# A new order table and new choices among equal engines in an attention and feed-forward kernel on one core

## The chip, the core and the metric

The kernel runs on one core of a Trainium2 chip. A core has five engines that work side by side, each through its own queue of instructions: TensorE (PE in the profile) multiplies matrices, VectorE (DVE), ScalarE (ACT) and GpSimd (POOL) work on elements, and SyncE (SP) here issues the transfers (DMA). Instructions of different engines wait for one another on semaphores. The metric is the device time of one execution in microseconds. The kernel before takes 1097.91 us (median of three runs, 1097.19 to 1097.92).

## The reference

Two parts follow one another. The first is attention with a threshold, over 8 batches, 8 heads, 576 positions and 64 channels a head; q, k and v are float32:

```python
scores = scale * np.matmul(q, k.transpose(0, 1, 3, 2))
thresh = np.max(scores, axis=-1, keepdims=True) - tau
scores = np.where(scores >= thresh, scores, -1000000000.0)
scores = scores - np.max(scores, axis=-1, keepdims=True)
attn = np.exp(scores)
attn = attn / (np.sum(attn, axis=-1, keepdims=True) + 1e-09)
return np.matmul(attn, v).astype(np.float32)
```

Its output, with the heads side by side, is x of 4608 tokens by 512. The second part is a feed-forward layer whose weights come as float64 (w_in 512 x 2048, w_out 2048 x 512): h = x @ w_in; g = h where h >= 1, 0 where h <= -1, (h + 1)^2 / 4 between; the output is g @ w_out.

## The kernel before, in words

**Numbers.** Products are made in float16 with a high and a low part of each factor (three products, high by high, high by low and low by high). A helper on line 466 issues most matmuls, so the feed-forward products of both kinds stand under that line: with `ph` as output the product x @ w_in, 144 steps of 48 matmuls (or parts of it), with `acc` as output the product g @ w_out, 264 steps. The q and k of the first four head pairs, all of batch 0, are used in float32 as they come ("exact", `f32` in a row), so that no split stands ahead of the first scores.

**Weights.** They arrive in 16 blocks for w_in and 16 for w_out, 128 x 512 float64 or 0.524 MB each (line 839). The float64 words are turned into float32 on lines 845 to 874: a letter for each block in `SIGN` (A, D or N) says which engines do it (A: ScalarE twice and VectorE once; D: GpSimd, ScalarE, VectorE twice; N: ScalarE, GpSimd, VectorE). After scales that come from all blocks (sums on line 881), a letter in `CONV` says how a block is scaled and split into high and low parts (lines 920 to 958):

- A: ScalarE scales and rounds (lines 922 and 928), GpSimd subtracts. G: all three on GpSimd.
- D: GpSimd scales and rounds in one (line 936), VectorE makes the residual from the block in SBUF (line 939).
- P and Q: GpSimd as in D, TensorE makes the residual (line 942), and ScalarE (P, line 949) or VectorE (Q, line 947) reads it from PSUM. M: TensorE scales, ScalarE rounds, VectorE subtracts.

**q and k after batch 0.** They are loaded in head pairs into `raw` and scaled and split by `add_qk`. A letter of `QHOW` says how: P (GpSimd line 645, ScalarE line 651, GpSimd line 658) or D (ScalarE line 649, VectorE line 656). v is scaled on line 728 (GpSimd) with its residual on line 733 (VectorE) for 28 head pairs; the first come as float32.

**Attention.** The scores are made in 288 tiles of 128 rows by 576 columns, two tiles to a visit (144 visits). `PAIR` says whether TensorE makes both tiles interleaved (J, one step) or one after the other (S, two steps) on line 1073. Each tile then goes: row maximum (VectorE line 1127), threshold (one column; VectorE line 1134, or ScalarE line 1132 where `THR` says A), exponential (ScalarE line 1137), mask and sum (VectorE line 1151), and then by its letter in `TILE`:

- P, where no letter stands: 1/sum (VectorE line 1161), norm (GpSimd line 1169), high part (ScalarE line 1177), low part (GpSimd line 1180).
- N: the same but the norm on ScalarE (line 1172), and VectorE's 1/sum has two short instructions (lines 1203 and 1204).
- V: high part with its norm on ScalarE (line 1207), low part on VectorE (line 1210). S is a form of V that works on the scores' own buffer (lines 1188 to 1199).

SyncE transposes the result (line 1213, tile `eT`), and TensorE multiplies it by v (line 1299). The sum goes to x on lines 1307 and 1311; x @ w_in goes through the gate on ScalarE and VectorE (lines 1376 to 1393), is multiplied by w_out and stored.

**Order.** All work is written down as 5016 operations on five engines, each with the operations that it follows and the buffers that it takes. The table `ORDER` lists them; `Plan.order` goes through the table, gives each operation its buffer slots and a planned time, and sorts by that. Each engine executes its operations in this sequence, so a step that waits holds all behind it on its engine. A last helper, `keep_warm` (line 1454), fills TensorE's planned gaps in the first 120 us with matmuls on a constant, 314 instructions before. The x @ w_in steps run through groups of 256 tokens: the first step of the second group is an event to which the prediction comes back, at 161.56 us.

Of the kernel before, what the change touches and what calls it, by code (L numbers as in the profile page):

```python
# [26 lines left out]
CONV = {"i": "AGAGGAGGPAGAADDP", "o": "PDDAADMGAAQGAGAD"}  # L27

SIGN = {"i": "NNNAADANAAANANAA", "o": "AAAANANAAANANNNN"}
THR = "VVAVVVVVVVAAVVAAAAAAAAAAVAVVVVAVVVAAVVAAVVAAVVVVAAAAVVAVVVVVVVVVVVVVVVVVVVVVVVVVVVVVVVVVVVVVVVVVVVVVVVVVVVVVVVVVVVVVVVVVVVVVVVVVVVVVVVVVVVVVVVVVVVVVVVVVVVVVVVVVVVVVVVVVVVVVVVVVVVVVVVVVVVVVVVVVVVVVVVVVVVVVVVVVVVVVVVVVVVVVVVVVVVVVVVVVVVVVVVVVVVVVVVVVVVVVVVVVVVVVVVVVVVVVVVVVVVVVVVVVVVVVVVVV"  # L30
PAIR = "SJSJSJSSJSSSSJJJJJSJJJJJJJJJJJJSJJJJJJJJJJJJJJJJJJJJJJJJJJJJJJJJJJJJJJJJJJJJJJJJJJJJJJJJJJJJJJJJJJJJJJJJJJJJJJJJJJJJJJJJJJJJJJJJJJJJJJJJJJJJJJJJ"
QHOW = "DDPDPPDPPPDDPPPPPPPPPPPPPDDPPPPP"
# [216 lines left out]
TILE = {3: "S", 5: "N", 8: "N", 18: "V", 20: "N", 22: "N", 25: "V", 26: "N", 27: "N", 29: "V", 30: "N", 32: "N", 55: "V", 69: "V", 71: "V", 94: "V", 114: "V", 117: "V", 150: "V", 152: "V", 173: "V", 181: "V", 186: "V", 200: "V", 214: "S", 222: "V", 257: "V", 262: "V", 287: "V"}  # L249
# [1261 lines left out]
```

## Time and profile before

| | |
|---|---|
| time, median of three runs | 1097.91 us |
| span of the profiled execution | 1097.3 us |
| TensorE busy | 1073.0 us (98%) |
| TensorE weight loads | 790.6 us (72%) |
| VectorE busy | 906.1 us (83%) |
| ScalarE busy | 871.2 us (79%) |
| GpSimd busy | 759.4 us (69%) |

The profiled execution has no other time than its span, which lies 0.6 us under the median. A busy share over the whole span mixes stages: the weights are converted only at its start, the attention ends well before its end, and TensorE's busy time contains the filler matmuls. It must be read by stretches of time, and the waits too.

### The profile page before, as it was taken

What the parts mean: (1) busy time and instruction counts of PE and PEld (TensorE: products, weight loads), DVE (VectorE), ACT (ScalarE), POOL (GpSimd) and SP (SyncE); (2) the same over time, 40 slices, a digit from 0 to 9 for tenths busy, and PEclk for the clock granted to TensorE, in tenths of its full rate; (3) what the DMA queues carried; (4) which work ended last, traced back from release to release, by engine and by line L of the source; (5) the groups of instructions that cost most, each with busy time, mean ns of one, the idle gap of its engine ahead of it and who ended that gap; (6) DMA issues with size and microseconds to landing.
All of it is one profiled execution on the core that took longest, in us unless ns stands there. A gap on an engine that the chain in (4) does not pass through costs nothing.

```text
span 1097.3 us, 36713 instructions
## 1 busy us (share of the span) xinstructions
PE 1073.0 (98%) x14591; PEld 790.6 (72%) x14591; DVE 906.1 (83%) x2651; ACT 871.2 (79%) x1682; POOL 759.4 (69%) x880
## 2 busy tenths in 40 slices
PE   8799999999999999999999999999999999999998
PEld 7477668777777777776777677777786677767774
DVE  5899999999888888988898998888887899877223
ACT  5999989897888897887798888778788986776333
POOL 5999998786678785897668776576567885565000
PEclk9799999999999999999999999999999999999999
DMA  9997899775977887787778788569856676557000
GB/s 352 332 256 143 139 188 141 152 140 115 191 140 141 152 152 127 135 150 137 139 142 146 150 128 147 113 127 164 151 102 120 131 128 127 105 95 132 18 15 20
DMA packets 420668, 155.88 MB, mean 142 GB/s; under 512 B 399504, under 2 KB 399504, under 8 KB 420496
## 3 DMA queue, kind: packets, MB, share of 16 engines
q1 hardware_dynamic: 420416, 153.41, 71.7%
q8 instruction: 114, 1.87, 0.7%
q14 instruction: 58, 0.48, 0.2%
q10 hardware_dynamic: 80, 0.13, 0.0%
HBM read 45.09 MB, written 9.44 MB: 50 GB/s over the span
## 4 chain that ended last, share of the span: by engine, by line
PE 80%; DVE 10%; DMA 5%; POOL 2%; issue 2%; ACT 1%; SPq 0%; DVEq 0%; POOLq 0%; ACTq 0%
PE acc L466 30%; PE ph L466 30%; PE s L1073 9%; PE ph L1299 9%; DMA eT<-hl 2%; DVE s L1127 2%; DVE e L1151 2%; POOL hl L1180 1%; PE ph L1454 1%; DMA qq<-in_q_dram 1%; DMA kk<-in_k_dram 1%; DMA raw<-in_v_dram 1%; DVE ph L1383 1%; POOL e L1169 0%; DVE WO L939 0%
## 5 line engine op out<-in xcount | busy, mean ns | idle before, releaser
L466 PEld LDWEIGHTS <-WI 128*64 128x64 f16 (+1 forms) x7446 | 407.3, 108 | 55.1 <-issue 18.3
L1180 POOL TENSOR_TENSOR hl<-e,hl 128x576 f16<-128x576 f32 x267 | 347.3, 1309 | 107.7 <-ACT hl L1177 101.8
L466 PE MATMUL ph<-x,WI 128*64 128x256 f16 (+1 forms) x6912 | 400.6, 264 | 2.3 <-DVE x L1311 0.9
L1169 POOL TENSOR_SCALAR e<-e,sm 128x576 f32<-128x576 f32 x259 | 203.5, 790 | 106.6 <-DVE sm L1161 75.3
L1151 DVE SCALAR_TENSOR_TENSOR e<-s,sm,e 128x578 f32<-128x578 f32 x286 | 229.9, 812 | 21.6 <-ACT e L1137 17.0
L1137 ACT ACTIVATE e<-s,sm 128x576 f32<-128x576 f32 x288 | 208.5, 739 | 40.4 <-DVE s L1127 36.4
L1127 DVE TENSOR_SCALAR_CACHE_REDUCE s<-s,pc 128x576 f32<-128x576 f32 x252 | 203.5, 820 | 36.6 <-PE s L1073 35.3
L1177 ACT ACTIVATE hl<-e 128x576 f16<-128x576 f32 x267 | 178.2, 680 | 44.1 <-POOL e L1169 41.1
L466 PE MATMUL acc<-WO,ga 128*64 128x512 f16 (+1 forms) x1590 | 203.4, 380 | 0.0
L1073 PE MATMUL s<-kk,qq 64*128 64x288 f16 (+3 forms) x1840 | 152.1, 300 | 9.9 <-DMA qq<-in_q_dram 5.2
L466 PEld LDWEIGHTS <-ga 128*64 128x64 f16 (+1 forms) x1590 | 91.2, 109 | 82.3 <-issue 9.9
L1383 DVE SCALAR_TENSOR_TENSOR ph<-ph,fcs,asq 128x512 f32<-128x512 f32 (+1 forms) x160 | 111.7, 700 | 46.1 <-ACT asq L1379 44.9
L1376 ACT ACTIVATE asq<-ph,fcs 128x512 f32<-128x512 f32 (+1 forms) x160 | 116.1, 736 | 37.7 <-PE ph L466 36.9
L1299 PE MATMUL ph<-eT,vst 128*64 128x320 f16 (+2 forms) x1928 | 122.7, 279 | 2.9 <-DMA eT<-hl 2.0
L1299 PEld LDWEIGHTS <-vst 128*64 128x64 f16 x1928 | 100.2, 110 | 22.9 <-issue 7.9
L1073 PEld LDWEIGHTS <-qq 64*128 64x128 f16 (+1 forms) x1680 | 66.2, 96 | 48.3 <-issue 35.6
L1388 ACT ACTIVATE ga<-ph,fcs 128x256 f16<-128x256 f32 (+1 forms) x160 | 70.2, 450 | 29.2 <-DVE ph L1383 22.4
L1379 ACT ACTIVATE asq<-asq 128x512 f32<-128x512 f32 x144 | 90.3, 629 | 3.2
L1393 DVE SCALAR_TENSOR_TENSOR ga<-ph,fcs,ga 128x256 f16<-128x256 f32 (+1 forms) x160 | 70.5, 449 | 23.7 <-ACT WI L1388 8.3
L466 PE MATMUL acc<-WO,gb 128*64 128x512 f16 (+1 forms) x546 | 71.0, 379 | 0.0
L466 PE MATMUL acc<-WO 128*64 128x512 f16 (+1 forms) x546 | 69.4, 380 | 0.0
L466 PE MATMUL acc<-WO,WI 128*64 128x512 f16 (+1 forms) x534 | 68.2, 380 | 0.0
(189 smaller groups left out, 1162.5 us busy)
## 6 DMA issues: line engine op xcount, KB each, us to landing
raw<-in_v_dram SPq DMA_DIRECT2D x32, 288.0 KB, 3.5
WO<-in_moe_w_in_dram SPq DMA_DIRECT2D x16, 512.0 KB, 8.6
out_dram<-ob SPq DMA_DIRECT2D x32, 256.0 KB, 2.8
raw<-in_q_dram SPq DMA_DIRECT2D x28, 288.0 KB, 3.4
raw<-in_k_dram SPq DMA_DIRECT2D x28, 288.0 KB, 3.5
x<-in_moe_w_out_dram SPq DMA_DIRECT2D x10, 512.0 KB, 7.0
eT<-hl SPq DMA_TRANSPOSE x288, 3.5
WO<-in_moe_w_out_dram SPq DMA_DIRECT2D x4, 512.0 KB, 4.3
```

The source lines that it names most:

```text
L466: T.matmul(out[x], lhsT[:, x], rhs, **flags)
L1073: T.matmul(ap(sb, s_ps)[r, f, :SH], q, k, start=ql == kl == 0, stop=exact or ql == 1)
L1127: V.tensor_scalar(sv(), sv(), c, None, ALU.mult, ALU.min, accum_out=t[:, 0:1])
L1137: A.activation(ev(), sv(), AF.Exp, bias=ap(m, sm)[:, 0:1], scale=-1.0)
L1151: V.scalar_tensor_tensor(ev(SH + 1), sv(SH + 1), t[:, 2:3], ev(SH + 1), ALU.is_le, ALU.mult, accum_out=t[:, 3:4])
L1169: G.tensor_scalar(ev(), ev(), ap(m, sm)[:, 5:6], ESC, ALU.mult, ALU.mult)
L1177: A.activation(part2(0), ev(), AF.Copy)
L1180: G.tensor_tensor(part2(w), ev(), part2(0), ALU.subtract)
L1299: T.matmul(o[hd * D : (hd + 1) * D, :n], vt[:, k, hd * D : (hd + 1) * D], t[:, kb, (hd ^ p % 2) * n : ((hd ^ p % 2) + 1) * n], start=m == ...
L1376: A.activation(tv()[:, :, c], hv()[:, :, c], AF.Relu, bias=fcs[:, b, 2, q : q + 1], scale=fcs[:, b, 3, q : q + 1])
L1379: A.activation(ap(tb, asq), ap(tb, asq), AF.Square)
L1383: V.scalar_tensor_tensor(hv()[:, :, c], hv()[:, :, c], fcs[:, b, 0, q : q + 1], tv()[:, :, c], ALU.max, ALU.min)
```

## The change

The table of all 5016 operations is another one, the letters of which engine does an operation are others, and `QHOW` now has one letter for q and one for k of each head pair where it had one for both. No operation and no buffer is new in kind. Of `ORDER`, which is 198 lines of numbers, the first line stands here; of `THR` 23 of its letters change (26 letters A before, 27 after), and it is left out.

```diff
-CONV = {"i": "AGAGGAGGPAGAADDP", "o": "PDDAADMGAAQGAGAD"}
-SIGN = {"i": "NNNAADANAAANANAA", "o": "AAAANANAAANANNNN"}
+CONV = {"i": "AGAGGAGGPAGAADDP", "o": "QDAAADMGGAQGAGAD"}
+SIGN = {"i": "NNAAADNNAAAAANAA", "o": "AADANANAAANANNNN"}
...
-PAIR = "SJSJSJSSJSSSSJJJJJSJJJJJJJJJJJJSJJJJJJJJJJJJJJJJJJJJJJJJJJJJJJJJJJJJJJJJJJJJJJJJJJJJJJJJJJJJJJJJJJJJJJJJJJJJJJJJJJJJJJJJJJJJJJJJJJJJJJJJJJJJJJJJ"
-QHOW = "DDPDPPDPPPDDPPPPPPPPPPPPPDDPPPPP"
+PAIR = "SSSSSJSSJSSSJSJJJJJJJJJJJJJJJJJJJJJJJJJJJJJJJJJJJJJJJJJJJJJJJJJJJJJJJJJJJJJJJJJJJJJJJJJJJJJJJJJJJJJJJJJJJJJJJJJJJJJJJJJJJJJJJJJJJJJJJJJJJJJJJJJJ"
+QHOW = "DDDDPPDDPPPPDPPPPPPPDPPPPPDPPPPDPPPPPPPPDDPPPPPPPPDDDDPPPPPPPPPP"
...
-    0, 605, 606, 607, 608, 609, 12, 16, 13, 17, 1, 14, 18, 15, 19, 20, 21, 590, 592, 22, 23, 595, 580, 582, 591, 585, 587, 2, 593, 600, 611, 616, 596,
+    585, 12, 16, 14, 0, 1, 13, 15, 17, 586, 587, 588, 18, 19, 20, 590, 21, 591, 22, 23, 39, 605, 592, 593, 606, 607, 608, 40, 24, 41, 42, 43, 580,
...
-TILE = {3: "S", 5: "N", 8: "N", 18: "V", 20: "N", 22: "N", 25: "V", 26: "N", 27: "N", 29: "V", 30: "N", 32: "N", 55: "V", 69: "V", 71: "V", 94: "V", 114: "V", 117: "V", 150: "V", 152: "V", 173: "V", 181: "V", 186: "V", 200: "V", 214: "S", 222: "V", 257: "V", 262: "V", 287: "V"}
+TILE = {3: "S", 5: "N", 8: "N", 18: "V", 20: "N", 22: "N", 25: "V", 26: "N", 27: "N", 29: "V", 30: "N", 32: "N", 37: "N", 55: "N", 62: "N", 65: "N", 69: "V", 71: "V", 72: "N", 73: "V", 85: "N", 90: "N", 94: "V", 96: "N", 99: "N", 101: "V", 107: "N", 109: "N", 110: "V", 111: "N", 114: "V", 117: "V", 119: "N", 146: "V", 147: "N", 151: "N", 153: "N", 154: "V", 157: "N", 164: "N", 173: "V", 174: "N", 181: "V", 186: "V", 200: "V", 214: "S", 222: "V", 257: "V", 262: "V", 287: "V"}
...
-            for how in plan.ways(("qk", at), QHOW[at], "PD"):
+            for how in plan.ways(("qk", 2 * at + n), QHOW[2 * at + n], "PD"):
```

Counted by instructions: line 1169 goes from 259 to 238, line 1172 from 8 to 27, lines 1203 and 1204 from 27 to 48, lines 1207 and 1210 from 19 to 21, line 1177 from 267 to 265, the fillers of line 1454 from 314 to 310; line 939 from 6 to 5 (on w_out from 4 to 3), line 947 from 1 to 2, line 949 from 3 to 2, line 874 from 1 to 2. `QHOW` has 46 letters P and 10 letters D on q and k after batch 0, in both kernels. TensorE's useful matmuls are the same. Of the 717 steps on TensorE about 217 stand elsewhere, none by more than 16 places.

Three places in the new order follow, each before and after. The first is SyncE's queue at its start. `WO` in a load is the buffer of a weight block, `x` also holds weight blocks at first, `kk` and `qq` are k and q of a head pair, `tcs` is the constant tau. Before:

```order
L571 DMA kk_76<-in_k_dram 128x576
L571 DMA qq_80<-in_q_dram 128x576
L839 DMA WO<-in_moe_w_in_dram 128x1024 x3
L571 DMA qq_81<-in_q_dram 128x576
L571 DMA kk_77<-in_k_dram 128x576
L839 DMA WO<-in_moe_w_in_dram 128x1024
L839 DMA x_107<-in_moe_w_out_dram 128x1024
L839 DMA x_105<-in_moe_w_out_dram 128x1024
L839 DMA WO<-in_moe_w_in_dram 128x1024 x3
L571 DMA kk_78<-in_k_dram 128x576
L571 DMA qq_82<-in_q_dram 128x576
```

After:

```order
L839 DMA WO<-in_moe_w_in_dram 128x1024 x7
L571 DMA kk_76<-in_k_dram 128x576
L571 DMA qq_80<-in_q_dram 128x576
L513 DMA tcs<-in_tau_dram 128x1
L839 DMA WO<-in_moe_w_in_dram 128x1024
L571 DMA qq_81<-in_q_dram 128x576
L571 DMA kk_77<-in_k_dram 128x576
L839 DMA WO<-in_moe_w_in_dram 128x1024 x3
L839 DMA x_107<-in_moe_w_out_dram 128x1024
L571 DMA qq_82<-in_q_dram 128x576
L571 DMA kk_78<-in_k_dram 128x576
```

The third pair's q (`qq_82`) stood behind 17 weight loads (8 of them stand ahead of the first row shown) and now stands behind 13 (one ahead of the first row); the four that were ahead now come later.

The second place is VectorE's queue at about 100 to 110 us of the trace of before, where w_out is split: line 939 makes a residual of a block, line 947 reads one from PSUM, line 1127 and 1151 are the maxima and masks of tiles, 1383 is a gate step, 1311 the low part of x. Before:

```order
L1151 SCALAR_TENSOR_TENSOR e_90,sm_126<-s_62,sm_126,e_90 128x578
L1311 SCALAR_TENSOR_TENSOR x_103<-ph_63,x_103 128x128
L939 SCALAR_TENSOR_TENSOR WO<-WO,wsc_o 128x512
L1161 RECIPROCAL sm_126<-sm_126 128x1
L1127 TENSOR_SCALAR s_61,sm_125<-s_61,tcs 128x2x288
L1127 TENSOR_SCALAR s_62,sm_127<-s_62,tcs 128x2x288
L939 SCALAR_TENSOR_TENSOR WO<-WO,wsc_o 128x512
L1210 SCALAR_TENSOR_TENSOR hl_96<-e_91,sm_123,hl_96 128x576
L1151 SCALAR_TENSOR_TENSOR e_89,sm_125<-s_61,sm_125,e_89 128x578
```

After:

```order
L947 TENSOR_SCALAR WO<-ph_64 128x512
L1151 SCALAR_TENSOR_TENSOR e_89,sm_125<-s_61,sm_125,e_89 128x578
...
L1311 SCALAR_TENSOR_TENSOR x_103<-ph_65,x_103 128x128
L1210 SCALAR_TENSOR_TENSOR hl_94<-e_92,sm_123,hl_94 128x576
L1127 TENSOR_SCALAR s_61,sm_127<-s_61,tcs 128x2x288
L1383 SCALAR_TENSOR_TENSOR ph_63<-ph_63,fcs,asq_101 128x512
L1127 TENSOR_SCALAR s_62,sm_126<-s_62,tcs 128x2x288
L1151 SCALAR_TENSOR_TENSOR e_92,sm_127<-s_61,sm_127,e_92 128x578
L1161 RECIPROCAL sm_127<-sm_127 128x1
L939 SCALAR_TENSOR_TENSOR WO<-WO,wsc_o 128x512
L1151 SCALAR_TENSOR_TENSOR e_90,sm_126<-s_62,sm_126,e_90 128x578
```

One of the two residuals of line 939 is gone from this stretch, and one more of line 947 stands some rows ahead.

The third place is TensorE's queue around the attention product that begins at 414.10 us of the trace of before. `s` is a score tile's PSUM buffer, `eT_98` the transposed tile, `vst_86` v, `WI` and `WO` hold weights in a feed-forward product and `gb_114` a gated result. Before:

```order
L466 LDWEIGHTS WI
L466 MATMUL ph_65<-x_104,WI 64x2x128
L1073 LDWEIGHTS qq_81
L1073 MATMUL s_61<-kk_77,qq_81 128x288
...
L1299 LDWEIGHTS vst_86
L1299 MATMUL ph_63<-eT_98,vst_86 64x256
...
L466 LDWEIGHTS WO
L466 MATMUL acc<-WO 64x512
```

After:

```order
L1073 LDWEIGHTS qq_81
L1073 MATMUL s_61<-kk_77,qq_81 128x288
L466 LDWEIGHTS gb_114
L466 MATMUL acc<-WO,gb_114 64x512
...
L466 LDWEIGHTS WO
L466 MATMUL acc<-WO 64x512
L466 LDWEIGHTS WI
L466 MATMUL ph_63<-x_104,WI 64x2x128
...
L1299 LDWEIGHTS vst_86
L1299 MATMUL ph_65<-eT_98,vst_86 64x256
```

Before, x @ w_in steps, a score pair, the attention product and then three accumulations (36 matmuls into `acc`) follow one another. After, the score pair comes first, then the three accumulations, then one step of x @ w_in, then the attention product.

## Rows read from the trace of the kernel before

**Rows 1.** Windows: stretch, length, engines' busy us (instructions), granted clock, DMA, GB/s.

```profile
25.00:161.60 136.60, 121.99 (x1415) 86.94 (x1416) 126.73 (x376) 127.63 (x254) 130.64 (x154) 0.95 0.96 216
161.60:606.30 444.70, 442.47 (x6271) 329.10 (x6271) 397.45 (x1180) 373.62 (x726) 336.97 (x374) 1.00 0.79 144
606.30:1097.30 491.00, 486.47 (x6672) 355.65 (x6668) 369.92 (x1063) 357.07 (x680) 279.68 (x303) 1.00 0.60 109
```

**Rows 2.** Chain of waits, 0 to 165 us: start, length, what.

```profile
26.52 9.13 DMA qq<-in_q_dram
...
161.56 3.49 PE ph L466 x65
```

**Rows 3.** Instructions by line and form: busy us, mean ns, idle us ahead.

```profile
L1169 POOL TENSOR_SCALAR e<-e,sm 128x576 f32<-128x576 f32 x259 | 203.5, 790 | 106.6 <-DVE sm L1161 75.3 <-ACT junk L685 5.7 <-ACT e L1137 4.2
...
L1134 DVE TENSOR_SCALAR sm<-sm,tcs 128x1 f32<-128x1 f32 x262 | 53.6, 211 | 6.3
...
L728 POOL TENSOR_SCALAR vb<-raw,scs 128x1152 f16<-128x1152 f32 x28 | 34.9, 1246 | 3.4 <-DVE scs L718 2.4 <-DVE e L1151 0.6 <-DMA vst<-vb 0.4
...
L733 DVE SCALAR_TENSOR_TENSOR vb<-raw,scs,vb 128x576 f16<-128x576 f32 x28 | 30.5, 1088 | 0.0
...
L1172 ACT ACTIVATE e<-e,sm 128x576 f32<-128x576 f32 x8 | 6.2, 770 | 0.0
...
L939 DVE SCALAR_TENSOR_TENSOR WO<-WO,wsc_o 128x512 f16<-128x512 f32 x4 | 5.9, 1463 | 0.1
...
L939 DVE SCALAR_TENSOR_TENSOR WI<-WI,wsc_i 128x512 f16<-128x512 f32 x2 | 1.6, 804 | 0.0
...
L874 DVE SCALAR_TENSOR_TENSOR WI<-WO,ph 128x512 uint32<-128x512 uint32 x1 | 0.7, 686 | 0.0
...
L947 DVE TENSOR_SCALAR WO<-ph 128x512 f16<-128x512 f32 x1 | 0.7, 671 | 0.0
```

**Rows 4.** Windows: around the wait for the third pair's q.

```profile
30.00:50.00 20.00, 12.64 (x76) 8.88 (x73) 17.65 (x51) 19.70 (x34) 19.49 (x23) 0.68 1.12 315
35.00:40.00 5.00, 4.22 (x18) 3.01 (x19) 4.16 (x11) 5.00 (x10) 4.58 (x8) 0.50 1.38 382
45.00:50.00 5.00, 5.00 (x37) 3.95 (x35) 3.86 (x9) 4.82 (x8) 5.00 (x7) 0.50 1.22 237
```

**Rows 5.** Waits over the whole span: us, times, longest.

```profile
PE s L1073 <- DMA qq<-in_q_dram: 5.2, 1, 5.2
ACT ph L853 <- DMA WO<-in_moe_w_in_dram: 4.4, 1, 4.4
...
ACT junk L685 <- DMA raw<-in_v_dram: 1.4, 1, 1.4
```

**Rows 6.** Timeline of TensorE: exact score pairs, start, length, idle ahead.

```profile
35.78 3.27 PE L1073 MATMUL s<-kk,qq 64*128 64x288 f32 x8 [5.21 <-DMA qq<-in_q_dram]
...
52.00 1.97 PE L1073 MATMUL s<-kk,qq 64*128 64x288 f32 x8 [0.28 <-DVE e L1151]
```

**Rows 7.** Two rows of the chain of waits, then two of TensorE's timeline.

```profile
188.28 2.62 PE ph L466 x48
...
191.74 2.74 PE ph L466 x48
...
224.54 1.17 PE L1073 MATMUL s<-kk,qq 64*128 64x288 f16 x12
...
402.44 0.91 PE L1073 MATMUL s<-kk,qq 64*128 64x288 f16 x12
```

**Rows 8.** TensorE's waits from 161.6 to 606.3 us, then two rows of its timeline.

```profile
PE ph L1299 <- DMA eT<-hl: 1.6, 3, 0.8
PE s L1073 <- DVE e L1151: 0.5, 2, 0.3
...
414.10 1.72 PE L1299 MATMUL ph<-eT,vst 128*64 128x256 f16 x28 [0.54 <-DMA eT<-hl]
...
585.71 2.09 PE L1299 MATMUL ph<-eT,vst 128*64 128x320 f16 x28 [0.80 <-DMA eT<-hl]
```

More of the change, by code (lines that the diff above doesn't have):

```diff
@@ L25 @@
 XJ, XS = 1.2, 1.0
-CONV = {"i": "AGAGGAGGPAGAADDP", "o": "PDDAADMGAAQGAGAD"}
-SIGN = {"i": "NNNAADANAAANANAA", "o": "AAAANANAAANANNNN"}
-THR = "VVAVVVVVVVAAVVAAAAAAAAAAVAVVVVAVVVAAVVAAVVAAVVVVAAAAVVAVVVVVVVVVVVVVVVVVVVVVVVVVVVVVVVVVVVVVVVVVVVVVVVVVVVVVVVVVVVVVVVVVVVVVVVVVVVVVVVVVVVVVVVVVVVVVVVVVVVVVVVVVVVVVVVVVVVVVVVVVVVVVVVVVVVVVVVVVVVVVVVVVVVVVVVVVVVVVVVVVVVVVVVVVVVVVVVVVVVVVVVVVVVVVVVVVVVVVVVVVVVVVVVVVVVVVVVVVVVVVVVVVVVVVVVVV"
-PAIR = "SJSJSJSSJSSSSJJJJJSJJJJJJJJJJJJSJJJJJJJJJJJJJJJJJJJJJJJJJJJJJJJJJJJJJJJJJJJJJJJJJJJJJJJJJJJJJJJJJJJJJJJJJJJJJJJJJJJJJJJJJJJJJJJJJJJJJJJJJJJJJJJJ"
-QHOW = "DDPDPPDPPPDDPPPPPPPPPPPPPDDPPPPP"
+CONV = {"i": "AGAGGAGGPAGAADDP", "o": "QDAAADMGGAQGAGAD"}
+SIGN = {"i": "NNAAADNNAAAAANAA", "o": "AADANANAAANANNNN"}
+THR = "AVAVVVVVVVVAVAAAAAAAAAAAAVVVAAAAAAVVVAVVVVVAVVVVVAVVVAVAVVVVVVVAVVVVVVVVVVVVVVVVVVVVVVVVVVVVVVVVVVVVVVVVVVVVVVVVVVVVVVVVVVVVVVVVVVVVVVVVVVVVVVVVVVVVVVVVVVVVVVVVVVVVVVVVVVVVVVVVVVVVVVVVVVVVVVVVVVVVVVVVVVVVVVVVVVVVVVVVVVVVVVVVVVVVVVVVVVVVVVVVVVVVVVVVVVVVVVVVVVVVVVVVVVVVVVVVVVVVVVVVVVVVVVVV"
+PAIR = "SSSSSJSSJSSSJSJJJJJJJJJJJJJJJJJJJJJJJJJJJJJJJJJJJJJJJJJJJJJJJJJJJJJJJJJJJJJJJJJJJJJJJJJJJJJJJJJJJJJJJJJJJJJJJJJJJJJJJJJJJJJJJJJJJJJJJJJJJJJJJJJJ"
+QHOW = "DDDDPPDDPPPPDPPPPPPPDPPPPPDPPPPDPPPPPPPPDDPPPPPPPPDDDDPPPPPPPPPP"
 EXPM = 0x7F000000
```

400 rows, old and new, of the table ORDER are left out of this document.

## The prediction

> **What bounds the kernel now.** I read the busy time of the engines by stretch first [rows 1]. From 161.60 us on TensorE leads alone: it is busy for 442.47 of 444.70 us up to 606.30, and for 486.47 of 491.00 after that, while VectorE, ScalarE and GpSimd each have over 47 us to spare in the first of these. Between 25 and 161.60 us it is otherwise: VectorE has 126.73, ScalarE 127.63 and GpSimd 130.64 of 136.60 us filled, and TensorE 121.99, part of it at half clock. So the kernel has two halves with different limits. The first converts weights, q, k and v and does the first softmax tiles, and three engines fill it together; the second is a queue of matmuls with nearly no gap. The chain of waits says where the one gives way to the other [rows 2]: the loads of k and q stand in it up to 35.65 us (the last piece is 9.13 us of the q load from 26.52), and at 161.56 us the chain enters the first product of the feed-forward part (x times w_in, line 466) for the second group of 256 tokens and stays on TensorE.
>
> From this comes the form of the sum. The end is the start of that product (161.56 us), plus the work of TensorE behind it, plus the waits of TensorE behind it. TensorE's order of instructions is the same, name for name, in both kernels from a point that lies at 606.3 us in the trace of before, and on the three other engines from about 618 us. A change of speed there is not to be expected, and everything has to come from before.
>
> **What the change does to the first half.** I add up what each engine executes ahead of the product at 161.56 us, in the old order and in the new one, and price what differs by the mean times of before [rows 3].
> VectorE: the residual of w_out block 2 leaves it (line 939, 1463 ns; form D becomes A, all on ScalarE and GpSimd), that of block 0 comes to it, read from PSUM (line 947, 671 ns; form P becomes Q); one residual of v (line 733, 1088 ns) and three threshold instructions net (line 1134, 3 x 211 = 633 ns) come later or go to ScalarE; one more step of bit work (line 874, 686 ns) comes in. That is 671 + 686 - 1463 - 1088 - 633 = -1827 ns, so -1.8 us. A tile whose norm goes to ScalarE needs two short VectorE instructions in place of one, and that adds a few tenths at most.
> ScalarE: what comes in (a norm of 770 ns on line 1172, one more bit step, three thresholds, the steps of block 2) and what goes out (two casts of q or k, block 0's residual, one step of line 853) nearly cancel. I take +0.2 us, and count it as 0.2.
> GpSimd: one v scaling (line 728, 1246 ns) comes after the product and one norm (line 1169, 790 ns) has gone to ScalarE; the steps of weight work cancel within some tenths. -2.0 us.
> No one of the three has 10 us of slack in the 136.60, and each passes work to the other two, so I move the product by their mean, (-1.8 + 0.2 - 2.0) / 3 = -1.2 us. The bounds are 0 (ScalarE, whose work is unchanged, sets the pace alone) and -2.0 (GpSimd, the fullest, does).
>
> In SyncE's queue q and k of the third head pair now stand behind 13 weight loads instead of 17. Four blocks of 0.524 MB at 382 GB/s (the rate from 35 to 40 us) [rows 4] are 5.5 us, and TensorE's longest wait is 5.2 us for just that q [rows 5]. That wait should go. I give it no gain, since the three other engines are filled in these 20 us but for VectorE, which has 20.00 - 17.65 = 2.35 us idle [rows 4]: what arrives early finds them occupied with weights. The four blocks that now land 2 to 5 us later are the other side of it; ScalarE once waited 4.4 us for such a block [rows 5]. One v load now stands behind four transposes of the queue as well; ScalarE waited 1.4 us for a v load already [rows 5].
>
> After the wait TensorE runs at a granted clock of 0.50, the 1.2 GHz level, from 35 to 40 and again from 45 to 50 us [rows 4]: the exact product of a pair takes 3.27 us there against 1.97 at 52.00 us [rows 6], which is 1.3 us for one pair and about 2.6 for two. The Trainium skill says the same in "TensorE: Matmul & The Clock Gate", section "HAM oscillation — how this bites in real kernels": an idle wait for data sends the engine back to its lower rate, and the cost is paid anew at every such wait. The trace agrees with the order of things, idle 5.21 us, then 0.50. By that rule a wait that only moves takes its slow products with it, and one that goes gives up to 2.6 us of TensorE time back; on TensorE alone, which waits for the others here, I count 0.
>
> The Trainium skill, "SBUF — State Buffer", section "Who interferes with whom", says that a VectorE instruction with two inputs in SBUF and a GpSimd instruction that reads SBUF block each other whole. The trace is in favour: line 939 takes 1463 ns on four w_out blocks in the crowded stretch and 804 ns on two w_in blocks of the same shape [rows 3]. By it, an instruction of line 939 fewer would also free GpSimd by up to the 0.66 us of difference, an estimate; my sum stays with the durations of rows.
>
> **What it does behind 161.56 us.** Three things. First, the work itself. A block of 48 matmuls of line 466 takes 2.62 us, or 2.74 where the array's shape is changed ahead of it [rows 7]. The new order changes shape 245 times there, not 247: -0.24 us. One pair of score tiles goes from "one after the other" (1.17 us) to interleaved (0.91 us) [rows 7]: -0.26. Together -0.5.
> Second, the waits. TensorE loses 1.6 us in three waits for a transpose and 0.5 in two for a masked tile [rows 8]. The largest but one, 0.54 us at 414.10, is that of the attention product of line 1299: in the new order three accumulations (36 matmuls of line 466, three times 1.3 us from start to start) stand ahead of it instead of behind it, so its transpose has 3.9 us more, and the wait goes. The two for a tile, together 0.5, should go because VectorE has some 3 us less ahead of it. The 0.8 us at 585.71 [rows 8] and the third (what is left of the 1.6, some 0.3) have the same neighbours as before and stay. -1.0 us, with bounds of 0 (each place is replaced by another) and -2.1 (all go).
> Third, the 19 tiles that newly take their norm on ScalarE instead of GpSimd, 18 of them behind 161.56 us. One costs ScalarE 770 ns [rows 3], or 18 x 0.77 = 13.9 us in all, and ScalarE has 444.70 - 373.62 = 71 us there [rows 1]; GpSimd loses as many norms of 790 ns. The few tiles that change to or from the third form (lines 1207 and 1210) come to two more in all. VectorE gets one short instruction more per tile and has 47 us. TensorE hides this whole edit. If the cover failed, a tile would be late by less than a microsecond at its own place, which the bounds of the waits hold. The threshold's 23 letters and the ten head pairs' q and k that change places with the same total are hidden alike.
>
> **Sum.** -1.2 - 0.5 - 1.0 = -2.7 us. The profiled execution spans 1097.3 us, and the median shown is 1097.91, 0.6 more; I add the same 0.6. 1097.9 - 2.7 = 1095.2 us. A measurement of this kernel tells about 0.2% from no change, which is 2.2 us here: faster means under 1095.7, slower over 1100.1.
>
> **Rivals.**
> (A) The forecast, 1095.2, its own range 1093.3 to 1096.9 (front -2.0 to 0, work -0.5, waits -2.1 to -0.5). Chance 0.45.
> (B) The first half keeps its length, because ScalarE's work is the same and it passes the beat to the others. Then only the work of TensorE and half of the waits go: 1097.9 - 0.5 - 0.5 = 1096.9. For it: ScalarE is busy in 19.70 of the 20 us from 30 to 50 [rows 4]. Against it: GpSimd is fuller over the whole stretch, and loses 2 us. Chance 0.25.
> (C) Slower. The four weight blocks deferred behind q and k leave ScalarE and VectorE without work between 20 and 45 us, and the wait of 5.2 us, gone from TensorE, stands on ScalarE, all of whose later work then comes late to 161.56 us. 1097.9 + 5.2 - 0.5 - 1.0 = 1101.6. It decides if ScalarE has less than 5.2 us of other ready work when the four blocks would have landed. For it: its 4.4 us wait for one such block [rows 5]. Against: exponentials and splits of the tiles that q and k bring earlier are that other work. Chance 0.16.
> (D) More than forecast: the wait for q does lie on the way. Its removal fills VectorE's 2.35 us of idle time between 30 and 50 us, on top of the rest: 1097.9 - 2.35 - 2.7 = 1092.9. For it: the chain of waits runs through that q load [rows 2], and VectorE's idle time lies in the half-clock stretches, where it waits for scores. Against: GpSimd is busy for 19.49 of the 20 us, with work that is only reordered. Chance 0.14.
> That the change doesn't do what it says is small: engines and orders do differ as described, only the letters for q and k have the same totals on either side (46 and 10 where they apply).
>
> **How the numbers follow.** The likeliest case gives 1095.2. The range of 8 in 10 takes the whole of A and B, the lower part of D and not C's middle: 1091.5 to 1100.0; A's own stands above. Under 1095.7 lie some 0.6 of A, a fifth of B and D whole: 0.28 + 0.05 + 0.14 = 0.47. Over 1100.1 lies C, with a hundredth for waits that I don't see: 0.17. The rest, 0.36, is within 0.2%.
>
> **What would show it.** Right: the first x times w_in product of the second token group starts 1 to 2 us earlier than 161.56; TensorE's 5.2 us wait for q at 30 to 36 us is gone or under 1 us; the wait of the attention product that stood at 414.10 is gone, that at 585.71 still there; the distance from 606.3 us to the end is the same to 0.3 us. Wrong: a ScalarE wait for a weight load longer than 4.4 us, or any stretch after 161.56 us in which TensorE is under 99% busy; and if the second half's length changes by over 2 us, the sum was put in the wrong place altogether.

## The result, and the profile after

The changed kernel is slower: 1112.83 us (median of four runs, 1112.63 to 1114.81) against 1097.55 (1096.71 to 1097.92), a ratio of 1.0144 [1.0130, 1.0159], or +15.3 us. The forecast was 1095.2 and the range ended at 1100.0. The time lies outside it on the other side, and beyond the slower rival C too (1101.6).

The time lies 1.8 us over the span in every execution for which both are known (1112.66 and 1110.9 for the profiled one of after). The profiled execution of before, with its span of 1097.3, was thus one of about 1099.1 us (an estimate from that difference), and not 0.6 under the median as the prediction took it. The two spans differ by 13.6 us where the medians differ by 15.3. I account for the 13.6.

The windows of after, cut at the same steps as [rows 1] and then at the same times as [rows 4] (length, busy us of PE, PEld, DVE, ACT and POOL with instructions, granted clock, DMA, GB/s):

```profile
25.00:166.00 141.00, 126.26 (x1427) 90.26 (x1426) 127.20 (x372) 128.76 (x255) 130.65 (x148) 0.95 0.94 212
166.00:618.70 452.70, 445.26 (x6289) 334.08 (x6289) 402.12 (x1198) 385.52 (x742) 317.42 (x355) 1.00 0.75 141
618.70:1110.90 492.20, 486.81 (x6672) 356.24 (x6668) 371.32 (x1069) 358.44 (x680) 279.97 (x306) 1.00 0.60 110
30.00:50.00 20.00, 15.34 (x107) 11.00 (x107) 16.15 (x48) 15.86 (x29) 16.77 (x21) 0.74 0.96 267
35.00:40.00 5.00, 5.00 (x20) 2.85 (x19) 2.94 (x7) 3.64 (x7) 4.28 (x5) 0.50 0.89 354
```

The first product of the second token group starts at 166.00 us and not at 161.56 (+4.4); from there to the step that stood at 606.3 it takes 452.7 and not 444.7 (+8.0); the rest takes 492.2 and not 491.0 (+1.2). Two things stand out. In the first stretch the three element engines are as busy as before (127.20, 128.76 and 130.65 us, each within 1.2 of [rows 1]) in 4.4 us more: nearly all that has come in is idle time, not work. From 30 to 50 us it shows: 16.15, 15.86 and 16.77 us busy where [rows 4] has 17.65, 19.70 and 19.49. The mean granted clock of the stretch is 0.95 in both, so it is not more time at the lower rate either; what differs is where that time falls and who waits for it. In the middle TensorE is no longer nearly full: 452.70 - 445.26 = 7.4 us are free, 2.2 before.

TensorE's timeline of after in the first stretch (start, length, what, idle ahead and what ended it):

```profile
34.28 2.25 PE L1073 MATMUL s<-kk,qq 64*128 64x288 f32 x4 [3.62 <-DVE e L1151]
37.01 2.29 PE L1073 MATMUL s<-kk,qq 64*128 64x288 f32 x4
...
40.49 2.34 PE L1454 MATMUL ph<-ones 128*128 128x128 bf16 x20
...
72.04 2.84 PE L466 MATMUL ph<-x,WI 128*128 128x128 f16 x48
...
166.00 4.21 PE L466 MATMUL ph<-x,WI 128*64 128x256 f16 x74
```

The wait of 5.2 us for the third pair's q [rows 5, 6] is gone, as forecast. In its place stands one of 3.62 us for a score buffer that VectorE's mask (line 1151) has to free, and behind it TensorE is granted 0.50 just as it was behind the old wait: the 1.2 GHz level. The other engines now stand idle for what TensorE makes at that rate. ScalarE's and VectorE's waits of after from 0 to 110 us:

```profile
ACT ph L853 <- PE ph L789: 1.8, 1, 1.8
ACT e L1137 <- DVE s L1127: 1.7, 2, 0.9
DVE s L1127 <- PE s L1073: 2.0, 2, 1.0
```

They end at 42.86 us (behind a small sum that TensorE makes), at 37.55 and 40.31 (maxima of scores) and at 36.58 and 39.33 us (the scores themselves).

TensorE's waits of after from 166.0 to 618.7 us (us in all, times, longest), which answer to the first two rows of [rows 8]:

```profile
PE ph L1299 <- DMA eT<-hl: 2.2, 4, 0.8
PE s L1073 <- DVE e L1151: 2.0, 4, 1.2
PE ph L1299 <- DVE ph L1383: 0.8, 1, 0.8
PE ph L466 <- DVE WI L1393: 0.8, 1, 0.8
PE ph L466 <- ACT junk L601: 0.5, 1, 0.5
PE acc L466 <- ACT ob L1438: 0.5, 1, 0.5
```

And some of those places in TensorE's timeline of after. The third row answers to 414.10 of [rows 8], the last to 585.71:

```profile
306.32 0.89 PE L1073 MATMUL s<-kk,qq 64*128 64x288 f16 x11 [1.22 <-DVE e L1151]
...
396.36 0.26 PE L466 MATMUL ph<-pc,sel 128*64 128x2 bf16 x6 [0.76 <-DVE WI L1393]
...
430.03 1.70 PE L1299 MATMUL ph<-eT,vst 128*64 128x256 f16 x28
...
437.44 1.72 PE L1299 MATMUL ph<-eT,vst 128*64 128x256 f16 x28 [0.85 <-DVE ph L1383]
...
596.40 3.81 PE L1299 MATMUL ph<-eT,vst 128*64 128x256 f16 x56
```

All four waits that the prediction gave a time or a tile have gone, 585.71 too, which was to stay. But 12 others stand in the list, 6.8 us in all where there were 2.1. That is +4.7 of the +8.0. Most of the other 3 us stands as longer busy time at TensorE (445.26 against 442.47): the same 708 score matmuls take 55.8 us where they took 54.9, the same 814 of the attention products 55.6 where they took 54.7, and x @ w_in takes no more. The rest I did not take apart.

The lines whose engine changed, by form in after (busy us, mean ns, idle ahead), for [rows 3]:

```profile
L1169 POOL TENSOR_SCALAR e<-e,sm 128x576 f32<-128x576 f32 x238 | 188.6, 796 | 118.3 <-DVE sm L1161 75.4 <-ACT hl L1177 8.4 <-ACT junk L685 5.7
...
L1172 ACT ACTIVATE e<-e,sm 128x576 f32<-128x576 f32 x27 | 20.9, 775 | 3.1 <-DVE sm L1204 3.0
```

The durations are those I used (775 ns for a norm on ScalarE, 770 before). New is the idle time ahead of line 1172, 3.0 us for VectorE's line 1204, where [rows 3] has 0.0: the norm on ScalarE waits at the head of its queue.

### The profile page after: what moved, and what is told of

Same layout as the page of the kernel before. It is cut to its first block, busy times and chain, and to the rows that moved or that the text cites. A ratio compares the mean times of both kernels' runs of the same rounds, so it can differ in the third digit from the quotient of the medians.

```text
span 1110.9 us, 36783 instructions
## 1 busy us (share of the span) xinstructions
PE 1080.1 (97%) x14608; PEld 798.6 (72%) x14608; DVE 912.9 (82%) x2674; ACT 885.7 (80%) x1701; POOL 741.0 (67%) x859
## 4 chain that ended last, share of the span: by engine, by line
PE 63%; DVE 8%; POOL 6%; DMA 4%; ACT 4%; issue 3%; SPq 0%; DVEq 0%; POOLq 0%; ACTq 0%
PE acc L466 25%; PE ph L466 24%; PE ph L1299 7%; PE s L1073 7%; POOL hl L1180 3%; DVE e L1151 2%; DMA eT<-hl 2%; DVE s L1127 2%; POOL e L1169 1%; ACT e L1137 1%; DMA raw<-in_k_dram 1%; DVE ph L1383 1%; ACT hl L1177 1%; DMA vst<-vb 1%; DVE vb L733 0%
## 5 line engine op out<-in xcount | busy, mean ns | idle before, releaser
L466 PEld LDWEIGHTS <-WI 128*64 128x64 f16 (+1 forms) x7488 | 411.6, 108 | 54.4 <-issue 15.5
L1180 POOL TENSOR_TENSOR hl<-e,hl 128x576 f16<-128x576 f32 x265 | 340.8, 1295 | 110.5 <-ACT hl L1177 108.4
L1169 POOL TENSOR_SCALAR e<-e,sm 128x576 f32<-128x576 f32 x238 | 188.6, 796 | 118.3 <-DVE sm L1161 75.4
L1073 PE MATMUL s<-kk,qq 64*128 64x288 f16 (+3 forms) x1840 | 156.2, 298 | 10.2 <-DVE e L1151 9.4
L466 PEld LDWEIGHTS <-ga 128*64 128x64 f16 (+1 forms) x1596 | 93.5, 109 | 80.2 <-issue 10.2
L1299 PE MATMUL ph<-eT,vst 128*64 128x320 f16 (+2 forms) x1928 | 125.0, 280 | 9.4 <-DMA eT<-hl 4.5
L1299 PEld LDWEIGHTS <-vst 128*64 128x64 f16 x1928 | 103.1, 111 | 27.9 <-issue 14.6
L466 PE MATMUL acc<-WO,WI 128*64 128x512 f16 (+1 forms) x576 | 72.4, 379 | 0.5 <-ACT ob L1438 0.5
L466 PE MATMUL acc<-WO 128*64 128x512 f16 (+1 forms) x516 | 65.2, 380 | 0.0
```

Source lines behind the costliest of these rows:

```text
L466: T.matmul(out[x], lhsT[:, x], rhs, **flags)
L1073: T.matmul(ap(sb, s_ps)[r, f, :SH], q, k, start=ql == kl == 0, stop=exact or ql == 1)
L1169: G.tensor_scalar(ev(), ev(), ap(m, sm)[:, 5:6], ESC, ALU.mult, ALU.mult)
L1180: G.tensor_tensor(part2(w), ev(), part2(0), ALU.subtract)
L1299: T.matmul(o[hd * D : (hd + 1) * D, :n], vt[:, k, hd * D : (hd + 1) * D], t[:, kb, (hd ^ p % 2) * n : ((hd ^ p % 2) + 1) * n], start=m == ...
```

## The experiments

Medians; before ran beside each, at 1097.5 to 1098.0 us. Their profiles can have other line numbers: in e1 to e4 lines 451, 1058, 1157, 1284 and 1378 are 466, 1073, 1172, 1299 and 1393 here.

**e1: the 19 norms back on GpSimd, the new order kept.**

```diff
-TILE = {... 37: "N", 55: "N", 62: "N", 65: "N", 72: "N", ...}
+TILE = {...}   # 19 letters N out; the tiles go back to form P
```

> The changed kernel (1112.8 us) with the 19 new norms of line 1172 given back from ScalarE to GpSimd (line 1169), order table unchanged. Theory 'norms': the 8 us that TensorE loses between the second group's first product and 619 us come from ScalarE, which got 19 x 0.77 = 14.6 us more; then 1104 to 1106 us. Theory 'order': they come from the places of the operations in the queues, the letters only follow; then 1111 to 1115 us, and the first half (166.0 us to that product) the same.

1123.95 us (ratio 1.0237 [1.0221, 1.0252]): 11 us more than after. Both theories missed. TensorE's waits from 160 to 640 us in e1 (the first row stands at 2.0 us in after):

```profile
PE s L1058 <- DVE e L1136: 8.6, 11, 2.3
PE ph L1284 <- DMA eT<-hl: 4.1, 6, 1.1
```

The new order needs the new norms: without them its score buffers come free late.

**e2: 18 of the norms alone, in the old order.**

```diff
+TILE = {... 37: "N", 62: "N", 65: "N", ...}   # in the kernel before
```

> The kernel before (1097.6 us) with 18 of the 19 norms moved to ScalarE in its old order table. Theory 'norms': 1103 to 1106 us. Theory 'order': ScalarE's 71 us of slack cover 18 x 0.77 = 13.9 us; 1097 to 1099 us.

1102.68 (1.0045 [1.0029, 1.0062]), +5.1. So this edit, which I had costed at nothing, is not free. Its timeline shows how (three engines, around 430 us):

```profile
428.50 0.78 ACT L1157 ACTIVATE e<-e,sm 128x576 f32<-128x576 f32 x1 [2.12 <-DVE sm L1189]
...
430.03 0.48 DVE L1378 SCALAR_TENSOR_TENSOR ga<-ph,fcs,ga 128x256 f16<-128x256 f32 x1 [1.42 <-ACT WI L1373]
...
430.96 2.81 PE L451 MATMUL ph<-x,WI 128*64 128x256 f16 x48 [1.56 <-DVE WI L1378]
```

The norm stands at the head of ScalarE's queue for 2.12 us, because VectorE has not yet made its 1/sum. The gate step behind it is late, VectorE waits 1.42 for that, and TensorE 1.56 for VectorE. In before GpSimd makes this norm, and what stands behind it in that queue from 424 to 431 us are norms, low parts and two instructions of 0.2 us.

**e14 and e15: one more instruction at the same 18 tiles of the kernel before, on VectorE (a short one) or on ScalarE (a copy in place, which waits for nothing new).**

```diff
-            V.reciprocal(t[:, 5:6], t[:, 3:4])
+            (j in MORE and V.tensor_scalar(t[:, 4:5], t[:, 3:4], 1.0 / ESC, None, ALU.mult)); V.reciprocal(t[:, 5:6], t[:, 3:4])
```

```diff
-            A.activation(part2(0), ev(), AF.Copy)
+            (j in MORE and A.activation(ev(), ev(), AF.Copy)); A.activation(part2(0), ev(), AF.Copy)
```

> The kernel before with one more short instruction on VectorE (about 0.15 us, on a column that nothing reads) at 18 tiles, those whose norm moved in the second run above; everything else as before. It is VectorE's share of that move without ScalarE's. The move cost 5.1 us. Theory 'VectorE is the limit of the middle': 18 x 0.15 = 2.7 us more on VectorE come out almost whole, 1099.5 to 1101 us. Theory 'ScalarE's place': VectorE's 47 us of idle time in the stretch take them, 1097.5 to 1098.5 us.

1097.83 (1.0001 [0.9992, 1.0011]): nothing.

> The kernel before with one more copy of the tile in place on ScalarE (0.7 us) just ahead of the high part at the same 18 tiles; the norm stays on GpSimd. It is ScalarE's share of the move, in volume. Theory 'ScalarE's place': what stands behind it in ScalarE's queue, exponentials among it, comes late, and TensorE waits: 1101 to 1104 us. Theory 'VectorE is the limit': ScalarE's 71 us of idle time take the 13 us, 1097.5 to 1099 us.

1100.47 (1.0026 [1.0015, 1.0037]): +2.7, between the two ranges expected. So VectorE's idle time does take its share, and ScalarE's takes its own only in part, although it has 71 us of it. About half of e2's 5.1 us is the ScalarE time itself; the other half I put down to the norm's own wait, which the copy does not have; no run separates that. TensorE's waits in e15 from 162 to 610 us:

```profile
PE s L1073 <- DVE e L1151: 1.7, 4, 0.9
PE ph L1299 <- DMA eT<-hl: 1.2, 2, 0.8
```

The first of them stood at 0.5 in [rows 8]: the mask that frees a score buffer comes later. From the end of a visit's scores to both of its masks e15 takes a mean of 4.99 us in this stretch, before 4.86.

**e3 and e4: the new order and letters ahead of the product at 161.56 us with the old ones behind it, and the reverse.**

```diff
 ORDER, letters of operations ahead of the product:  e3 after's,  e4 before's
 ORDER, letters of operations behind it:             e3 before's, e4 after's
```

> All operations that the new table has ahead of the second group's first product in the new order and with the new letters, all others in the old order with the old letters. Theory 'middle': the first half costs 4.4 us and the middle's own new order the rest; then 1097.6 + 4.4 = 1102 us with waits of TensorE behind the product near the 2 us of before. Theory 'debt': the new first half hands over softmax work that is late, and the waits of the middle come with it; then 1107 to 1113 us.

1110.26 (1.0128 [1.0100, 1.0156]). The product is 2.8 us late, and from 9 to 14 us behind it there is one large wait in e3's timeline:

```profile
178.40 5.33 PE L451 MATMUL ph<-x,WI 128*64 128x256 f16 x48 [5.04 <-DVE gb L1378]
```

Behind the wait TensorE is at 0.50 for these 48 matmuls, which take 5.33 us instead of 2.8. From there the distance to before stays at 9.5 to 10.7 us to the end. The old middle does not cure the new front. But TensorE has no wait over 1.3 us in the middle of after, so this one belongs to the seam of the two tables, and its 5 us are no part of the 15.3.

> The reverse: all that the old table has ahead of that product in the old order and letters, the rest in the new. Theory 'middle': 1112.8 - 4.4 = 1108 us, with 8 us of waits in the middle as in the changed kernel. Theory 'debt': 1097 to 1101 us.

1106.04 (1.0078 [1.0063, 1.0093]). The product is 0.8 us early, and the middle loses about 7 us all the same, with waits mostly at the same steps as in after. The new middle is slow with either front, so the front is not the whole cause.

**e5 and e6: in each gap of the queues, the exponential on ScalarE and the mask on VectorE ahead of the gate steps that stood before them (71 moves in after, 69 in before).**

```diff
 ScalarE
+L1137 exponential of the tile
 L1379 gate
 L1388 gate
-L1137 exponential of the tile
```

> The changed kernel; between the second group's first product (166 us) and 619 us, 71 exponentials (line 1137) and masks (line 1151) that were ready but stood behind other work on ScalarE or VectorE are moved ahead of that work; same letters, same instructions. Theory 'loop': two score buffers make TensorE wait for the mask of the tile before, and the new table puts more between maximum, exponential and mask (0.96 us of wait ahead of an exponential on average against 0.64 before), so the 8 us of the middle come back in part: 1105 to 1109 us. Rival 'volume': TensorE waits because the three engines have too much to do in all by then; a mere change of places gives nothing, 1111 to 1114 us.

> The same treatment of the kernel before (69 moves in the same stretch). Theory 'loop': TensorE waits only 2 us there, so 0 to 2 us are to be had, or some lost where the moved-back work becomes late: 1096 to 1099 us. Rival 'volume': no change, 1097 to 1098 us.

1124.15 (1.0241 [1.0225, 1.0256]) on after and 1102.73 (1.0043 [1.0026, 1.0059]) on before: worse both times, and both theories missed. Worked out from the starts and ends in the traces from 166 us to the end of the middle, the mean wait of a tile whose maximum is there for its exponential fell from 0.72 us in after to 0.33 in e5, but that for the mask rose from 0.61 to 0.92, and the buffers came free no sooner: 5.26 and 5.24 us from the end of the scores to both masks. (The 0.96 and 0.64 of the expectation come out as 0.72 and 0.48 in this count.) TensorE's waits in e5 from 166 to 620 us:

```profile
PE s L1073 <- DVE e L1151: 5.1, 11, 1.3
```

**e7, e11 and e12: the fillers of TensorE in the front.** e7 puts 58 fillers into the 3.62 us wait, e12 also 16 at about 41 us, e11 takes away the 20 at 40.49.

```diff
+        left.insert(11, (28.9, banks[2][2], 3.3))   # e7, e12
+        left.insert(13, (38.5, banks[2][2], 0.9))   # e12
+        left.pop(11)                                # e11 alone
```

> The changed kernel with 58 more filler matmuls (3.3 us) in TensorE's wait of 3.6 us at 30.7 us. Theory 'clock': the granted clock stays at 1.00 from 30 to 45 us, the exact score tiles take 1.2 instead of 2.3 us, and the first x times w_in product (72.0 us) starts 2 us earlier: 1110 to 1111 us. Rival 'elements': TensorE's rate is covered by the element engines in these stages; that product moves by less than 0.5 us, 1112 to 1114 us.

1117.15 (1.0169 [1.0139, 1.0199]), 4 us more than after. The slow spell only moved, to 42.9 to 49.7 us, and the fillers already there took longer in it: 4.23 us for 38, where the new ones ahead go in 3.97 us for 68 (e7's timeline):

```profile
31.24 3.97 PE L1454 MATMUL ph<-ones 128*128 128x128 bf16 x68
...
44.91 4.23 PE L1454 MATMUL ph<-ones 128*128 128x128 bf16 x38
```

> The changed kernel without one run of 20 filler matmuls, which took 2.34 us at half clock at 40.49 us; behind it a sum of the weights (line 789) waited that releases ScalarE (1.8 us) and VectorE (0.7 us). Theory 'slow spell': in the first half TensorE's work at half clock is what the three element engines wait for; the first x times w_in product comes 1.5 to 2 us earlier than 72.0 and the time falls to 1110.5 to 1111.5 us. Rival: that time is not on the way; 1112 to 1114 us.

1119.17 (1.0189 [1.0171, 1.0208]): the spell became longer, 0.50 from 35 to 50 us, against the direction expected.

> The changed kernel with 58 filler matmuls in the wait of 3.6 us at 30.7 us (as in the run before with these) and 16 more at about 41 us, so that TensorE does not rest between 28 and 45 us. Theory 'slow spell': the executions whose mean granted clock is 0.996 or more take 1110 to 1111.5 us, those with a lower one are longer by 1 to 2 us for each 0.001; the first x times w_in product starts by 70.5 us. Rival: time and clock are not tied, and the times lie at 1112 to 1118 us whatever the clock.

1110.97 (1.0118 [1.0101, 1.0135]). Windows and TensorE's timeline of e12:

```profile
30.00:50.00 20.00, 18.17 (x197) 13.87 (x196) 18.82 (x55) 18.62 (x33) 19.14 (x23) 1.00 0.96 290
```

```profile
34.23 1.21 PE L1073 MATMUL s<-kk,qq 64*128 64x288 f32 x4 [0.39 <-ACT hl L1196]
...
69.61 2.84 PE L466 MATMUL ph<-x,WI 128*128 128x128 f16 x48
...
162.75 5.41 PE L466 MATMUL ph<-x,WI 128*64 128x256 f16 x96
```

With the clock at 1.00 in this window, the score step that took 2.25 us takes 1.21 although it starts no sooner, the three element engines are filled again (18.82, 18.62 and 19.14 of 20 us), and the product starts 3.2 us earlier than in after. So this slow spell is worth 3.2 of the 4.4 us in the front. In the end only 1.9 of it is left, and the intervals of the two ratios overlap.

A second slow spell of after stands at 94.6 to 98.0 us, where before has none. Windows of before and after, then TensorE's timeline of after (two rows) and of e5 (two rows):

```profile
95.00:100.00 5.00, 4.49 (x61) 2.81 (x62) 4.81 (x19) 4.91 (x11) 4.75 (x9) 1.00 0.29 56
95.00:100.00 5.00, 5.00 (x79) 4.78 (x79) 3.09 (x11) 4.70 (x12) 3.94 (x8) 0.70 0.56 126
```

```profile
94.62 1.76 PE L1299 MATMUL ph<-eT,vst 128*64 128x128 f16 x29 [1.44 <-DMA eT<-hl]
96.31 3.63 PE L466 MATMUL ph<-x,WI 128*128 128x128 f16 x48
...
95.12 1.00 PE L1299 MATMUL ph<-eT,vst 128*64 128x128 f16 x29 [1.49 <-DMA eT<-hl]
96.05 2.85 PE L466 MATMUL ph<-x,WI 128*128 128x128 f16 x48
```

The profiled executions of e5, e3 and e13, which execute the same instructions in the same order as after up to the product, let it be priced. Without this spell the product starts at 165.13 (e5) and 164.38 us (e3), with 3.4 us of it at 166.00 (after), with 6.9 us of it at 167.73 (e13). So it costs after some 1 to 1.5 us, which is an estimate from four single executions; e12 still has it (from 91.0 to 94.4 us), and in e7 it is 6.8 us long.

In the old front such time is covered. The profiled executions of before, e14, e15, e6 and e4, with the same instructions in the same order up to the product (e14 has one more on VectorE), have 13.6 to 17.1 us at 0.50 ahead of it, and those with 17 us reach it no later (160.80 to 161.17 us) than those with 13.6 (160.60 and 161.56).

**e8: SyncE's first 32 operations in the old order, the rest as in after.**

```diff
-WO x7, kk_76, qq_80, tcs, WO, qq_81, kk_77, WO x3, x_107, qq_82, kk_78
+kk_76, qq_80, WO x3, qq_81, kk_77, WO, x_107, x_105, WO x3, kk_78, qq_82
```

> The changed kernel with SyncE's first 32 operations in the old order (q and k of the third head pair behind 17 weight loads again); all other queues as changed. Theory 'loads': the four weight blocks that now land later cost the first half its 4 us; then 1108 to 1110 us. Rival: the first half lost its time to the new places on the element engines, which now find a q that is late as well; 1112 to 1118 us.

1121.86 (1.0223 [1.0208, 1.0239]). The new loads fit the new queues better than the old ones do. It is no clean test of the four deferred blocks, and so of rival C, since the edit also changes which weight block comes first, and ScalarE waits for that one in e8 (its longest wait for a weight block in after is 4.2 us):

```profile
ACT ph L853 <- DMA WO<-in_moe_w_in_dram: 10.9, 1, 10.9
```

**e9 and e10: TensorE's order behind the product alone.** e9 gives before after's TensorE order there (with the one letter of `PAIR` that goes with it); e10 gives e4, the kernel with the old front and the new middle, before's. The other letters and queues stay.

```diff
 ahead of the product, all queues:             both before's, with more fillers
 TensorE's queue behind it:                    e9 after's,   e10 before's
 letters and all other queues behind it:       e9 before's,  e10 after's
```

> The kernel before, but behind the second group's first product TensorE takes its steps in the new table's order; letters and the queues of the four other engines are the old ones (four operations stand one place later so that no queue locks another). Theory 'early steps': the new table has score and attention steps earlier on TensorE than their inputs are ready, and the 6 to 7 us of the middle (seen with the old first half: 1106.0 against 1097.5 us) come with TensorE's order alone: 1103 to 1107 us. Rival 'late elements': they come from the element engines' queues and letters; then 1097.5 to 1099 us.

> The counterpart: old first half, and behind it the new letters and the new queues of VectorE, ScalarE, GpSimd and SyncE, with TensorE's steps in the old order (one step one place off). Theory 'early steps': near 1098 us. Rival 'late elements': 1103 to 1107 us. If both this and its counterpart are slow, order and letters hold only together.

1162.72 (1.0595 [1.0580, 1.0611]) and 1156.37 (1.0536 [1.0518, 1.0553]), far slower than either whole. The planned gaps that `keep_warm` fills have changed too: both hold 17 filler matmuls more than before ahead of the product and reach it 7.2 (e9) and 4.6 us (e10) late. The other 50 us and more come behind it. TensorE's waits there, e9 and then e10:

```profile
PE s L1073 <- DVE e L1151: 30.4, 24, 6.9
```

```profile
PE ph L1299 <- DVE WO L1393: 8.3, 4, 5.4
PE ph L466 <- ACT junk L685: 6.7, 1, 6.7
```

Each of the two TensorE orders is good only with the element queues it was made for.

**e13: six waiting steps of after put one place later** (three attention products, two steps of line 466 for sums, and one v residual of VectorE).

```diff
 TensorE
+L466 acc<-WO,ga_110 x12
 L1299 attention product (204.33 us)
-L466 acc<-WO,ga_110 x12
```

> The changed kernel with six steps put behind the next one on their own engine, just where TensorE waits for them in its trace: the attention products that begin at 204.33, 243.59 and 437.44 us (0.87, 0.69 and 0.85 us of wait) and the two small sums at 396.36 and 417.20 us (0.76, 0.52) behind the next product each, and on VectorE the residual of v (line 733) that ends at 305.21 us behind the mask that the score pair of 306.32 us waits for (1.26). Theory 'places': the middle's waits are single steps that stand one place too early, so most of these 5.0 us come back: 1108 to 1110 us. Rival 'one chain': the queues hold each other so closely that a wait taken away at one place stands up at the next; 1111.5 to 1115 us.

1111.60 (1.0123 [1.0108, 1.0138]): 1.2 us come back of the 5.0 that these six waits show, and the interval overlaps with that of after, so even these are not clear of noise. The wait moves on, as in this row of e13, next to 396.36 where after had 0.76:

```profile
398.42 2.81 PE L466 MATMUL ph<-x,WI 128*64 128x256 f16 x48 [0.75 <-DVE pc L632]
```

None of the fifteen beats the kernel before.

## Why the prediction was wrong

**The product at 161.56, "-1.2".** It is +4.4. The failed step is the one that moved the product by the mean change in work. None of the three engines is busy for over 1.2 us more, and the 1.8 and 2.0 us that were to leave VectorE and GpSimd do not show; what counted was idle time. The premise that "three engines fill it together" held for the old order only, where 3.4 us more at half rate delay nothing (e15, e6 and e4). In the new one the engines stand idle from 30 to 50 us for sums and scores that TensorE makes slowly. That weight work which had filled such gaps is no longer there to fill them is how I read it; no run tests that by itself.

**"I count 0" for the clock.** This is the term that was mis-sized: 3.2 of the 4.4 us are the first slow spell, by e12, and the second one, at 94.6 us, is worth about the rest. The prediction cited "TensorE: Matmul & The Clock Gate", section "HAM oscillation — how this bites in real kernels", of the Trainium skill, in the form that a wait that only moves takes its slow products with it. The trace agrees: 3.62 us idle, then 0.50, and 1.00 where e12 filled it. I had given the rule no sum because TensorE "waits for the others here"; but the others wait for TensorE's scores. The count of 0 fits the old order, whose engines were filled, and not the new one.

**"That wait should go. I give it no gain."** The q came in time and the wait did go. Missing was the question what is late next: the score buffer, 3.62 us.

**Waits behind 161.56, "-1.0", bounds 0 to -2.1.** They are +4.7 in the list of waits. The single statements held, at 414.10 and at the two tiles; 585.71 failed in my favour. What failed is the bound: "each place is replaced by another" assumed as many new waits as old, of the same size. Nothing in the profile of before limits them. A tile's loop with two score buffers had little to spare. Worked out from the starts and ends of the 66 visits of the middle in each trace, both buffers are free a median of 0.80 us before TensorE's next scores begin in before, and 0.44 in after; in 6 visits of before and 29 of after it is under 0.3 us. From the end of the scores to both masks it takes a mean of 4.86 and 5.26 us. The margin goes with the middle and not with the front (0.45 us in e4, 0.76 in e3), and the norms alone take part of it (0.61 in e2). With so little to spare small delays on ScalarE or VectorE become waits of TensorE: that fits all these traces, though no run changes the margin alone.

**The 19 norms, hidden by 71 us.** Wrong by e2: +5.1 in the old order, where I wrote that TensorE hides this whole edit. Idle time summed over 444.70 us is not slack for an instruction that must run in its place in the queue. What it waits for (2.12 us) and what stands behind it (gates, exponentials) decide. For VectorE's short instruction the cover held (e14). In the new order, though, the norms are needed (e1), so the 5.1 can't be counted as a part of the 15.3.

**TensorE's work, "-0.5".** It can't be seen apart from the 3 us of longer busy time. The rest behind 618.7, forecast as equal to 0.3 us, is 1.2 longer, of which about 0.6 comes at 924 us (with a 0.4 us wait for a transpose) and 0.5 at the very end.

**The signs of being wrong.** Two of the three that were named came: TensorE is busy for 98.4% of the stretch from 166.0 to 618.7 us, under the 99%, and the second half is 9.2 us longer where 2 was the limit. By the prediction's own words the sum was put in the wrong place.

**The rivals.** C had the sign, and ScalarE and VectorE do stand without work at times between 30 and 45 us, as it said; but no weight wait of ScalarE's stands there, and what they wait for is TensorE. A and B both took for granted that the middle could only gain. What none of them held is that the new order could be worse by its own making.

**What stays open.** e4 shows that the new middle costs some 7 us with either front. Which of its moves begins it is not found: e1, e5, e9 and e10 each exchange a piece and are slower, and e13, where a wait taken away stands up at the next step, speaks for one chain rather than a list of single waits. To go on I would move the scores of single visits, one at a time.

## What to carry to other kernels

Busy time summed over a stretch says what an in-order engine could hold, not what it hides: of each instruction moved to it, ask what it waits for and what is queued behind it. The number and size of the old waits do not bound what a new order can cost; look at the margin of the tightest loop too (here a median of 0.44 to 0.80 us for the score buffers). A slow stretch of one engine cost nothing here while the others had work to fill it (the old front), and up to 3.2 us where they waited for it (the new one). Order and engine choices stand or fall together: pieces of one table put into the other made kernels slower than either (e9, e10), so an edit's price in one order says little of its price in another.

## What the runs showed of the hardware that was not expected

With the new front the mean granted clock goes with the time from execution to execution of one kernel: e12 at .999, .998, .998 and .996 took 1110.28, 1110.83, 1111.11 and 1112.80 us; e7 at .997, .994, .994 and .992 took 1111.39, 1116.68, 1117.62 and 1119.32. Five thousandths of the mean clock go with 8 us there. In before it does not: 17 executions beside e14 and e15, at .991 to .994, took 1096.76 to 1099.98 us without relation to it; the shortest and the longest both stand at .992.

In e7 the rate fell at 42.9 us though no idle time of TensorE in the 12 us ahead was longer than 0.7 us. And the same wait in the same order can be followed by either rate: behind 1.44 us for a transpose at 94.62 us after went to 0.50, behind 1.49 us at 95.12 e5 stayed at 1.00. Why is not settled.

Fillers meant to keep the rate up cost twice as much once it has fallen (58 ns each at 31.24 us of e7, 111 ns at 44.91), and they hold up the real matmuls queued behind them.

The residual of line 939 takes 742 to 1792 ns in after for blocks of one shape. Its instructions (shortest, median and longest in ns, first and last start):

```profile
L939 DVE SCALAR_TENSOR_TENSOR WO<-WO,wsc_o x3: 742/1756/1792, 88.3 to 140.3; 128x512 f16<-128x512 f32 x3
L939 DVE SCALAR_TENSOR_TENSOR WI<-WI,wsc_i x2: 743/842/941, 63.3 to 70.1; 128x512 f16<-128x512 f32 x2
```

So the means of [rows 3] do not part w_out from w_in: the third w_out block, at 140.28 us, took 742 ns. The two long ones, at 88.30 and 110.24 us, began under 0.1 us behind a GpSimd subtraction of line 1180 (1.29 and 1.27 us long) and ended some 0.55 us behind its end; in e12 one that met two of these in a row took 3037 ns. "SBUF — State Buffer", section "Who interferes with whom", of the Trainium skill gives a reason, that such a VectorE instruction and a GpSimd instruction that reads SBUF block each other. The trace agrees with it in these durations.
